# A shorter last warm-up matmul and differently cut weight loads at the head and at the first W2 chunk of a gated attention and MLP kernel

## The chip, the cores and the metric

The kernel runs on one core of a Trainium2 chip. TensorE (PE) multiplies, VectorE (DVE) and ScalarE (ACT) work on whole tiles, GpSimd (POOL) does a little, SyncE (SP) mostly issues DMA transfers; ACT and POOL can issue them too. The metric is the device time of one execution in microseconds (us). Lower is better. Times of a kernel are the median of several executions; the profile is of one further execution.

## The reference

The input x has 2048 rows (tokens) of 512 values in bf16. Two branches are computed from it and mixed row by row with a gate:

```python
g = sigmoid((x * gate_w).sum(-1))
# A: linear attention, 32 heads of 16
q, k, v = split(x @ wqkv)
phi = lambda t: where(t > 0, t + 1, exp(t)) + 1e-6
kv, z = phi(k)^T v, sum_s phi(k)           # per head
a = ((phi(q) kv) / (phi(q) z + 1e-6)) @ wo
# B: an MLP over the tokens of the layer-normed x
u = gelu(einsum("bsd,sf->bdf", layernorm(x), w1) + b1)   # F = 1792
b = (einsum("bdf,fs->bds", u, w2) + b2).transpose
out = g * a + (1 - g) * b
```

## The kernel before, in words

All operands are cut into tiles of 128 partitions: x has NT = 16 row tiles of 128 tokens, D = 512 makes ND = 4 blocks, F = 1792 makes NF = 14. A schedule written out by hand gives the order of instructions on each engine; nothing is reordered. Each engine works its own list, and semaphores hold an instruction until what it reads is there.

**The head.** SP issues the loads of x's row tiles 0 and 1 (`load_x`, L126, 128 KB each into `xs`), ACT issues parts of Wk, the middle third of wqkv (`load_wk`, L129, 128 KB for one of the four blocks k of the contraction, into `wk_sb`), and SP issues Wk's last block. x is also wanted transposed, in `xT`. Tiles 2 to 15 come transposed by DMA (`load_xT`, L132, on SP, first three single tiles, then two and three at a time); tiles 0 and 1 are transposed on TensorE (`transpose_part`, L194: matmuls `pt` of an `xs` block with the identity), and copied out of PSUM by DVE or ACT (`copy_part`, L199). Before the first block of x is there, TensorE runs `warm_up(6)` (L184, L190): six matmuls of 128x512 on a constant into the bank `wps` that nothing reads. Behind its loads, ACT has the load of its function table and a one-column exponential `act_warm` (L189).

Then the row of work on TensorE is: four `pt` of tile 0; `k_part(0, ...)` with k = 0 and 1 (`kacc`, contraction block k of x's tile times `wk_sb[:, k]`); four `pt` of tile 1; tile 0's k = 2; tile 1's k = 0 and 1; tile 0's k = 3; tile 1's k = 2 and 3; and then tile after tile.

**The rest.** For each further row tile: four `kacc` matmuls (keys), phi on ACT and DVE, and four `gacc` matmuls (Gram matrix of x and phi(k), four tiles behind). Then 16 rounds of three `uacc` (first MLP layer, W1's first chunk) and four `qacc` matmuls (queries); the remaining eleven `uacc` blocks with the small attention matrices `kvps` and `w2ps` between them; and for each output tile four `aps` and fourteen `yps` matmuls, a mix on DVE and the output transfer.

**Order of transfers.** SP's list is: x and Wk of the head, the transposed and plain tiles of x in turn, wq, W1's first chunk, wv, wo, W1's other three chunks, then W2's four chunks (`load_w2`, L432, each into a buffer of the pool `wstream` that a W1 chunk held before), then the outputs. A W2 chunk (128 x 14 x 512, 1792 KB) is issued in two halves of seven blocks of F. The first waits for the matmuls `uacc` that read W1's first chunk. Loads issued by SP and ACT count their landings on eight counters that are taken in turn.

## Time and profile before

| | us |
|---|---|
| median of three runs | 163.08 |
| lowest and highest | 162.43, 163.41 |
| profiled execution, its own time | 162.26 |
| its span, first to last instruction | 160.6 |

| stretch of the profiled execution | from, us | what TensorE does there |
|---|---|---|
| warm-ups | 0.85 | six matmuls on a constant |
| tiles 0 and 1 of x | 3.36 | transposes and first `kacc` |
| keys and Gram matrix | 6.2 | `kacc` and `gacc` in turn |
| queries and first MLP blocks | 32.3 | `uacc` and `qacc` in turn |
| other MLP blocks | 56.5 | `uacc`, with `kvps` at 63.4 and `w2ps` at 64.65 |
| outputs | 95.6 | `aps` and `yps` in turn, until 157.8 |

A line of the profile's timeline gives start, length, engine, line of the kernel, operation, output and inputs, count, and in brackets how long the engine was idle before it and what released it. "PEld" is the load of a matmul's stationary operand, and a "q" behind an engine's name (ACTq, SPq) is its queue of DMA issues: the length there is the time that the issue takes, not the transfer. The time from an issue to the landing of all its data is listed apart.

### The profile page before, as it was taken

The page shows a single profiled execution, that of the slowest core. Times are in us where ns is not written, and L with a number is a line of the kernel's source. Part 1 is how long each engine was busy: PE and PEld are TensorE (multiplying, and loading weights), DVE is VectorE, ACT ScalarE, POOL GpSimd, SP SyncE. Part 2 cuts the span into 40 slices and gives each one's busy share as a digit, 9 for nine tenths or more (in the row PEclk, how much of TensorE's full clock was granted, in tenths as well). Part 3 has the DMA queues.
Part 4 walks back from the last instruction along what each step waited for, and adds up shares of the span by engine and source line. Part 5 has one row for each costly group of instructions (what it writes and reads, how often), then busy time and mean ns, then how long its engine had stood idle before and what let it go on. Part 6 is the DMA issues. An engine that isn't in the chain of part 4 may idle for free.

```text
span 160.6 us, 2228 instructions
## 1 busy us (share of the span) xinstructions
PE 155.9 (97%) x822; PEld 72.5 (45%) x836; DVE 124.3 (77%) x274; ACT 72.7 (45%) x113; POOL 7.3 (5%) x17
## 2 busy tenths in 40 slices
PE   7999999999999999999999999999999999999993
PEld 2444444444444445444444444444444444444462
DVE  1599999769999998756999999676999999711122
ACT  3543486654978393059873320237333442111110
POOL 3000332002010000000000000000000000000000
PEclk9999999999999999999999999999999999999999
DMA  5699999999970007600930679401000001110001
GB/s 168 150 231 262 328 352 329 354 349 348 336 171 0 0 0 257 204 0 4 356 101 2 213 244 306 151 33 37 33 33 33 33 33 58 48 61 33 33 33 33
DMA packets 29929, 23.07 MB, mean 144 GB/s; under 512 B 8384, under 2 KB 29888, under 8 KB 29920
## 3 DMA queue, kind: packets, MB, share of 16 engines
q1 hardware_dynamic: 29104, 22.15, 45.2%
q10 hardware_dynamic: 704, 0.66, 1.2%
q0 software_dynamic: 112, 0.14, 0.4%
q8 instruction: 6, 0.10, 0.3%
q14 instruction: 3, 0.02, 0.0%
HBM read 19.01 MB, written 2.10 MB: 131 GB/s over the span
## 4 chain that ended last, share of the span: by engine, by line
PE 84%; DVE 13%; issue 1%; ACT 0%
PE yps L110 30%; PE uacc L110 24%; PE kacc L110 9%; PE gacc L110 9%; PE aps L110 9%; DVE pqT L213 6%; DVE zacc L274 3%; DVE stats L233 2%; DVE e L210 2%; PE wps L110 2%; PE qacc L110 1%; DVE mv L234 1%; ACT e L209 0%; PE kvps L110 0%; PE w2ps L110 0%
## 5 line engine op out<-in xcount | busy, mean ns | idle before, releaser
L110 PE MATMUL uacc<-hs,w1c 128*128 128x512 bf16 (+1 forms) x227 | 50.8, 379 | 0.4 <-issue 0.2
L110 PE MATMUL yps<-uT,w2c 128*128 128x512 bf16 (+2 forms) x247 | 50.8, 355 | 0.3
L110 PEld LDWEIGHTS <-w2c 128*128 128x128 bf16 x252 | 23.6, 98 | 25.2
L110 PEld LDWEIGHTS <-w1c 128*128 128x128 bf16 (+1 forms) x233 | 21.8, 98 | 26.0 <-issue 0.2
L488 ACT ACTIVATE a_sc<-aps,c,gg 128x512 f32<-128x512 f32 x16 | 12.4, 775 | 31.2 <-PE aps L110 15.5
L501 DVE SCALAR_TENSOR_TENSOR ot<-yps,c,a_sc 128x512 bf16<-128x512 f32 (+2 forms) x18 | 12.3, 688 | 15.3 <-PE yps L110 11.7
L322 ACT ACTIVATE uT<-uacc,bcol 128x512 bf16<-128x512 f32 x14 | 9.3, 686 | 17.5 <-PE uacc L110 17.4
L110 PE MATMUL qacc<-xT,wq_sb 128*128 128x512 bf16 x64 | 16.4, 379 | 0.1
L110 PE MATMUL aps<-W2sb,pqT 128*128 128x512 bf16 x63 | 16.4, 379 | 0.1
L110 PE MATMUL kacc<-wk_sb,xT 128*128 128x512 bf16 x63 | 15.9, 379 | 0.2 <-DVE xT L205 0.2
L387 DVE STREAM_TRANSPOSE zT<-pz 128x512 f32<-128x512 f32 x16 | 11.3, 705 | 6.0 <-ACT pz L386 6.0
L110 PE MATMUL gacc<-pk,xs 128*128 128x512 bf16 x63 | 15.7, 379 | 0.1
L249 ACT ACTIVATE hs<-xs,nmr,rstd 128x512 bf16<-128x512 bf16 x16 | 12.8, 805 | 2.3 <-DVE nmr L243 2.3
L209 ACT ACTIVATE e<-kacc 128x512 bf16<-128x512 f32 x16 | 9.4, 594 | 9.7 <-PE kacc L110 8.5
L386 ACT ACTIVATE pz<-pqT,zcol 128x512 f32<-128x512 bf16 x16 | 11.4, 715 | 4.8 <-DVE ot L501 4.7
L209 ACT ACTIVATE e<-qacc 128x512 bf16<-128x512 f32 x16 | 9.5, 594 | 7.7 <-PE qacc L110 7.7
L396 DVE STREAM_TRANSPOSE rex<-rd 128x512 bf16<-128x512 bf16 x16 | 11.4, 711 | 0.6
L213 DVE SCALAR_TENSOR_TENSOR pqT<-qacc,e 128x512 bf16<-128x512 f32 x16 | 11.1, 692 | 0.6
L213 DVE SCALAR_TENSOR_TENSOR pk<-kacc,e 128x512 bf16<-128x512 f32 x16 | 11.1, 692 | 0.6
L389 DVE TENSOR_REDUCE den<-zT 128x32 f32<-128x512 f32 x16 | 11.0, 686 | 0.6
L210 DVE TENSOR_SCALAR e<-e 128x512 bf16<-128x512 bf16 x32 | 9.0, 282 | 2.5 <-ACT e L209 2.5
L233 DVE BATCH_NORM_STATS2 stats<-xs 128x6 f32<-128x512 bf16 x16 | 10.9, 683 | 0.0
(58 smaller groups left out, 96.2 us busy)
## 6 DMA issues: line engine op xcount, KB each, us to landing
w2c<-in_B_w_dram SPq DMA_DIRECT2D x8, 896.0 KB, 5.7
w1c<-in_B_w_dram SPq DMA_DIRECT2D x3, 2048.0 KB, 14.0
out_dram<-ot SPq DMA_DIRECT2D x13, 128.0 KB, 1.7
xs<-in_A_x_dram SPq DMA_DIRECT2D x1, 1024.0 KB, 6.6
w1c<-in_B_w_dram SPq DMA_DIRECT2D x1, 1024.0 KB, 15.3
xs<-in_A_x_dram SPq DMA_DIRECT2D x1, 512.0 KB, 5.0
wq_sb<-in_A_wqkv_dram SPq DMA_DIRECT2D x1, 512.0 KB, 5.6
wv_sb<-in_A_wqkv_dram SPq DMA_DIRECT2D x1, 512.0 KB, 12.3
```

The costliest lines, as they stand in the source:

```text
L110: nc.tensor.matmul(o, lhsT=lhsT, rhs=rhs, start=start, stop=stop, **kw)
L209: nc.scalar.activation(out=e[:], in_=acc[:], func=ACT.Exp)
L210: nc.vector.tensor_scalar(out=e[:], in0=e[:], scalar1=1.0, scalar2=PHI_EPS, op0=ALU.min, op1=ALU.add)
L213: nc.vector.scalar_tensor_tensor(out=dst, in0=acc[:], scalar=0.0, in1=e[:], op0=ALU.max, op1=ALU.add)
L233: nc.vector.bn_stats(out=stats[:], in_=xs[:, t, :])
L249: nc.scalar.activation(out=hs[:, t, :], in_=xs[:, t, :], func=ACT.Identity, scale=rstd[:, t : t + 1], bias=nmr[:, t : t + 1],)
L386: nc.scalar.activation(out=pz[:], in_=seg, func=ACT.Copy, scale=zcol[:, j : j + 1])
L387: nc.vector.transpose(out=zT[:], in_=pz[:])
L389: nc.vector.tensor_reduce(out=den[:], in_=zT[:].rearrange("p (a d) -> p a d", d=HEAD), op=ALU.add, axis=AX.X)
L396: nc.vector.transpose(out=rex[:].rearrange("p (a d) -> p a d", d=HEAD), in_=rd[:].unsqueeze(2).to_broadcast([P, SC // HEAD, HEAD]),)
L488: nc.scalar.activation(out=a_sc[:], in_=aps[:], func=ACT.Identity, scale=gg[:, t : t + 1], bias=c2[:, t : t + 1],)
L501: nc.vector.scalar_tensor_tensor(out=ot[:, :W], in0=yps[:, :W], scalar=c1[:, t : t + 1], in1=a_sc[:, cs], op0=ALU.mult, op1=ALU.add,)
```

## The change

Three edits. The first two blocks of Wk, one load of 256 KB on ACT's queue, become two loads of 128 KB, with a load of x's tile 1 (on SP) between them in program order; the order of the other two Wk loads in the text is swapped, and they are on different queues. The sixth warm-up matmul has 256 columns instead of 512. The first W2 chunk is loaded in one piece of 14 blocks.

```diff
     load_x(nc.sync, 0, 1)
-    load_wk(nc.scalar, 0, 2)
+    load_wk(nc.scalar, 0, 1)
     load_x(nc.sync, 1, 1)
+    load_wk(nc.scalar, 1, 1)
+    load_wk(nc.sync, 3, 1)
     load_wk(nc.scalar, 2, 1)
-    load_wk(nc.sync, 3, 1)
     for t in (2, 3, 4):
         load_xT(t, 1)
...
-    warm_up(6)
+    warm_up(5)
+    warm_up(1, SC // 2)
...
         w2c.append(w)
-        for f0 in (0, NF // 2):
-            f1 = f0 + NF // 2
+        n = NF if c == 0 else NF // 2
+        for f0 in range(0, NF, n):
+            f1 = f0 + n
```

The order of instructions on every engine is otherwise the same, with one load more at the head of ACT's list and one less among SP's W2 loads. Since the counters are taken in turn, each load behind the new one uses the next counter, and from the W2 loads on the numbering is as before.

## The prediction

> **What bounds the kernel now.** I read the totals first.

> ```profile
> span 160.6 us, 2228 instructions
> PE 155.9 (97%) x822; PEld 72.5 (45%) x836; DVE 124.3 (77%) x274; ACT 72.7 (45%) x113; POOL 7.3 (5%) x17
> ```

> TensorE is busy for 155.9 of 160.6 us, and the chain of waits agrees: PE holds 84% of it. DVE's 13% lie between 33.8 and 55.5 us, where PE is busy for 23.84 us of the 24 between 32 and 56, so PE is not held up there either. In the chain 20 gacc matmuls take 4.32 us and 14 yps matmuls 3.02 us: 0.216 us each, end to end. So the kernel is one gapless row of matmuls, and time can be won or lost only before that row closes up, or after it. The second view is therefore the timeline of PE at the head (start, length, work; in brackets the idle time before).

> ```profile
> 0.85 2.72 PE L110 MATMUL wps<-const-bfloat16-1.0 128*128 128x512 bf16 x6 [0.85 <-PEq L522]
> 3.36 0.53 PE L110 MATMUL pt<-ident,xs 128*128 128x128 bf16 x4
> 4.06 0.60 PE L110 MATMUL kacc<-wk_sb,xT 128*128 128x512 bf16 x2 [0.17 <-DVE xT L205]
> 4.50 0.39 PE L110 MATMUL pt<-ident,xs 128*128 128x128 bf16 x4
> 4.72 1.63 PE L110 MATMUL kacc<-wk_sb,xT 128*128 128x512 bf16 x6
> ```

> The weight loads, copies and issues of the same stretch, then the transfers (KB each and median us from issue to landing; the last line is for the two x loads):

> ```profile
> 3.19 0.53 PEld L110 LDWEIGHTS <-xs 128*128 128x128 bf16 x4 [0.53 <-DMA xs<-in_A_x_dram]
> 4.05 0.29 PEld L110 LDWEIGHTS <-xT 128*128 128x128 bf16 x2 [0.34 <-DVE xT L205]
> 4.32 0.39 PEld L110 LDWEIGHTS <-xs 128*128 128x128 bf16 x4
> ...
> 3.71 0.49 DVE L205 CAST xT<-pt 128x128 bf16<-128x128 f32 x2 [1.48 <-PE pt L110]
> 4.76 0.62 DVE L205 CAST xT<-pt 128x128 bf16<-128x128 f32 x2 [0.56 <-PE pt L110]
> ```

> ```profile
> 0.81 0.98 ACTq L129 DMA_DIRECT2D wk_sb<-in_A_wqkv_dram  x2
> 1.73 0.42 SPq L129 DMA_DIRECT2D wk_sb<-in_A_wqkv_dram  x1
> 2.20 5.26 SPq L132 DMA_TRANSPOSE xT<-in_A_x_dram  x4
> ...
> 1.82 1.28 ACT L189 ACT_TABLE_LOAD   x1 [1.82 <-issue]
> 3.11 0.20 ACT L189 ACTIVATE act_warm<-ones_f 128x1 f32<-128x1 f32 x1
> 3.93 0.38 ACT L203 ACTIVATE xT<-pt 128x256 bf16<-128x256 f32 x1 [0.61 <-PE pt L110]
> ```

> ```profile
> wk_sb<-in_A_wqkv_dram ACTq DMA_DIRECT2D x1, 256.0 KB, 3.1
> xs<-in_A_x_dram SPq DMA_DIRECT2D x2, 128.0 KB, 2.7
> wk_sb<-in_A_wqkv_dram ACTq DMA_DIRECT2D x1, 128.0 KB, 3.3
> wk_sb<-in_A_wqkv_dram SPq DMA_DIRECT2D x1, 128.0 KB, 3.3
> ...
> DMA to landing us min/median/max: 2.3/2.7/3.0
> ```

> The reader is to see three things. First, the sixth warm-up starts at 2.93 and, at the 0.43 us that its fellows stand apart, hands over at 3.36, though x's first block let the weight load go at 3.19. Second, landings come in order of issue: x0 0.81+2.3 = 3.11; Wk0-1 0.81+3.1 = 3.91; x1 1.27+3.0 = 4.27; Wk2 1.30+3.3 = 4.60; Wk3 1.73+3.3 = 5.03. In bytes: 128 KB at 3.11, 384 at 3.91, 512 at 4.27, 640 at 4.60, 768 at 5.03, so 0.33 to 0.43 us for each 128 KB; the engines are saturated (374 GB/s from 2.80 to 3.20). Third, Wk2 lands at 4.60 and is used at 4.72: it has 0.12 us to spare.

> **Part 1, the half warm-up.** It removes 256 of 512 columns: 0.43/2 = 0.21 us, so the sixth ends at 3.14 and the first transpose waits for x0's weight load at 3.19. How soon a matmul follows a load that nothing covers: 0.01 us where the load at 5.10 is followed by kacc at 5.11, 0.03 at the very first pair (0.82, 0.85), and no more than a whole slow load, 0.15. I take 0.03, the pair in the same slow stretch: first transpose at 3.22, 0.14 us earlier (bounds 0.02 and 0.17). The four transposes, the DVE copy and its weight load follow, so the first kacc could go at 4.06-0.14 = 3.92, and ACT's copy at 3.93-0.14 = 3.79.

> **Part 2, Wk in three loads on ACT's ring.** ACT issues three for two: 0.46 us for the first (until 1.27), 0.49 for the second (1.30), and the third, Wk2, at 1.79 instead of 1.30. The table load behind them slides by 0.49 to 2.31-3.59 and act_warm to 3.60-3.80: under ACT's copy at 3.79 but for 0.01, and it would cost only if the table load became slower. SP's order is unchanged: x0, x1, Wk3, then the transposing loads. New on SP: loads take eight completion counters in turn, so the ninth waits for the first. With one more load at the head that is now the third single-tile xT load (L132), waiting for Wk0. It was issued at 4.84 and Wk0 lands by 3.91, so nothing; behind it stand the rest of x, wq and W1, which would all be late if it did wait. From there each SP load waits for the one eight earlier, as before.

> Issue times now: Wk0 and x0 0.81, x1 1.27, Wk1 1.30, Wk3 1.73, Wk2 1.79. If landings keep that order and the byte table above holds: x0 3.11; Wk0 (256 KB) halfway from 3.11 to 3.91, 3.51; x1 (384) 3.91; Wk1 (512) 4.27; Wk3 (640) 4.60; Wk2 (768) 5.03. A landing lets an instruction go about 0.05 us later (x1: 4.27, load at 4.32). Walk PE: first kacc 3.92 (Wk0 is there). Second kacc wants 3.92+0.23 = 4.15, but Wk1 gives 4.32; before it started at 4.29. The lead of 0.14 is gone. Tile 1's transposes 4.32+0.22 = 4.54 (x1 is there), kacc for k=2 wants 4.76 but Wk2 gives 5.08 where before it went at 4.72. Then tile 1's first kacc, which has to wait for its DVE copy until 5.11+0.03 anyway, follows at 5.08+0.22 = 5.30: 0.19 us later than 5.11. Wk3, needed next at 5.73, has long landed; xT's tile 2 (2.20+3.5 = 5.7) is wanted at 6.2+0.19. From here PE has no gap that could take the 0.19 up, so it reaches the end.

> Bounds: the order of Wk1 against x1 (0.03 us apart in issue) and of Wk2 against Wk3 (0.06 apart) decides. If Wk1 and Wk2 come first in each pair, they land at 3.91 and 4.60; kacc goes at 4.15, x1 at 4.27 lets tile 1's transposes go at 4.37, k=2 at 4.65, and tile 1's first kacc at 5.11-0.14 = 4.97: the whole 0.14 stays (0.17 at the bound). If each order goes wrong and the extra load costs a further step of 0.05, the loss is 0.25. I take the order of issue, since all five landings of before keep it.

> **Part 3, first W2 chunk in one load.** One SP issue less (0.4 to 0.56 us) at 59.97. Its halves landed in 4.6 and 6.8 us; as one load of 1792 KB it lands in no more than W1's 2048 KB took, 14.0 us, so by 74. The first yps matmul is at 96.25: 22 us cover it; only a landing later than 96 would cost. The next issue on SP waits for uacc until 74.86 in any case. I take nothing, at both ends.

> **Sum** against the profiled execution, 162.26 us (span 160.6, 1.66 around it): +0.19 + 0 + 0 = 162.45. That execution is 0.82 below the median of the runs, 163.08; the same +0.19 there gives 163.27, forecast as 163.3.

> **The clock.** The row of granted clock shows full speed throughout, but the durations don't: warm-ups stand 0.43 us apart, later matmuls 0.216; tile 0's transposes take 0.53 us, tile 1's 0.39. So TensorE went from half to full pace between 3.6 and 4.06, some 2.8 to 3.2 us after its first matmul. [...]

> **Rivals.** (B) The lead survives. For it: Wk1 and x1 are issued within 0.03 us, Wk2 and Wk3 within 0.06. Also, where the pace switches over 1 us later, kacc takes 0.43 each, k=2 is wanted only after 5.1, and Wk2's landing hides. Against it: five of five landings in order of issue. It gives 162.26-0.14 = 162.12, by the runs 162.9.
> (C) The clock switches late: the slower one. Place: the hand-over at 3.14, where PE now pauses before x0, and again at 4.15 and 4.76 for Wk. It decides if these pauses (0.08+0.17+0.32 us) leave the stretch too idle for full pace. Price: another slow stretch of 2.8 to 3.2 us at half pace loses 1.4 to 1.6; with 1.5, 163.76, by the runs 164.6. For it: the runs of before already differ by 0.98 us (162.43 to 163.41), as a wandering switch would make them. Against it: the later two pauses come after the switch of the trace, and the first takes 0.08 us of about 3.
> (D) The change has no effect, 163.1: both halves cancel. It is the middle between A and B, and counted with them.

> **Numbers.** A difference under 0.5% (0.82 us) can't be told from none. A, the forecast, 0.54; B 0.30; C 0.16. Spread of the runs lets A fall 0.02 faster, 0.48 same, 0.04 slower; B 0.05, 0.25, 0; C 0, 0.04, 0.12. Together: faster 0.07, same 0.77, slower 0.16. A and B with their spread reach from 162.4 to 163.9, and leaving out most of C keeps it within 2 in 10.

> **What would show it.** Right: first transpose at about 3.22; an idle time of PE before the second kacc and a longer one before k=2, ended by a load of wk_sb; tile 1's first kacc near 5.30; the spacing 0.216 from there; W2's one load landed by 74. B: no wait on wk_sb, tile 1's first kacc near 4.97. C: matmuls 0.43 us apart beyond 5.5. Wrong altogether: PE waits for xT or hs later on, or a changed row after 60 us.

## The result and the profile after

The changed kernel takes 164.58 us in the median of 22 runs (163.14 to 165.61) against 162.77 of 22 (162.24 to 163.44) for the kernel before: a ratio of 1.0088, with a 95% interval of 1.0061 to 1.0115. (The ratios here and below lie near those of the means; the two medians alone give 1.0111.) It is slower. The medians hide the form: eleven of the runs lie between 163.14 and 164.09, eleven between 165.07 and 165.61, and none between. I call them the lower and the upper group; the kernel before has only one. So there are two losses to explain: some 0.6 us in the lower group (its median is 163.36), and 2 us more in the other half of the runs.

The profiled execution belongs to the lower group; at 163.14 us it is the fastest of all 22. Totals and chain of waits of the changed kernel, from its page:

```profile
span 161.3 us, 2242 instructions
PE 157.3 (98%) x836; PEld 72.6 (45%) x836; DVE 124.3 (77%) x274; ACT 72.7 (45%) x113; POOL 7.3 (5%) x17
...
PE 96%; DMA 2%; DVE 0%; issue 0%
```

The span grew by 0.7 us, and a DMA has come into the chain: the page's next line names the load of x, at 2%. The head of the changed kernel on the timeline of PE, and the weight loads there:

```profile
0.85 2.51 PE L110 MATMUL wps<-const-bfloat16-1.0 128*128 128x512 bf16 x6 [0.85 <-PEq L525]
3.66 0.61 PE L110 MATMUL pt<-ident,xs 128*128 128x128 bf16 x4 [0.31 <-DMA xs<-in_A_x_dram]
4.33 1.03 PE L110 MATMUL kacc<-wk_sb,xT 128*128 128x512 bf16 x2
5.16 0.46 PE L110 MATMUL pt<-ident,xs 128*128 128x128 bf16 x4
5.60 1.71 PE L110 MATMUL kacc<-wk_sb,xT 128*128 128x512 bf16 x7
```

```profile
3.66 0.34 PEld L110 LDWEIGHTS <-xs 128*128 128x128 bf16 x4 [1.00 <-DMA xs<-in_A_x_dram]
5.84 0.55 PEld L110 LDWEIGHTS <-xT 128*128 128x128 bf16 x4 [0.34 <-DVE xT L207]
```

The reader is to see that the first transpose starts at 3.66, not at 3.36 as before or 3.22 as forecast, because x's first block lands only at 3.62. Tile 0's k=2 starts at 5.60 (before 4.72), and tile 1's first kacc at 5.84 (before 5.11). That shift of 0.73 is the 0.7 by which the span grew, so nothing after it matters. What held that kacc back to the last was the copy of tile 1's transposes by DVE (the second weight load above), late because x was late and because nearly all of TensorE's work up to there ran at the slow pace. The first two kacc take 1.03 us together, where they took 0.60 before: TensorE is still at its slow pace there, which the profile of before had left by then. The transfers of the changed kernel (KB each, median us from issue to landing), the first three issued before 2.1 us, the last from the page:

```profile
wk_sb<-in_A_wqkv_dram ACTq DMA_DIRECT2D x3, 128.0 KB, 3.2
xs<-in_A_x_dram SPq DMA_DIRECT2D x2, 128.0 KB, 2.9
wk_sb<-in_A_wqkv_dram SPq DMA_DIRECT2D x1, 128.0 KB, 3.4
```

```profile
w2c<-in_B_w_dram SPq DMA_DIRECT2D x1, 1792.0 KB, 7.6
```

The three ACT loads took 3.0, 3.2 and 3.8 us; the last of them, Wk2, issued at 1.74, landed at 5.56. W2's one load, issued at 60.7, landed by 68.3 and was wanted at 97.0.

### The profile page after: what moved, and what is told of

The parts are those of the page before. It is cut to its first block, busy times and chain, and to the rows that moved or that the text cites. A ratio compares the mean times of both kernels' runs of the same rounds, so it can differ in the third digit from the quotient of the medians.

```text
span 161.3 us, 2242 instructions
## 1 busy us (share of the span) xinstructions
PE 157.3 (98%) x836; PEld 72.6 (45%) x836; DVE 124.3 (77%) x274; ACT 72.7 (45%) x113; POOL 7.3 (5%) x17
## 4 chain that ended last, share of the span: by engine, by line
PE 96%; DMA 2%; DVE 0%; issue 0%
PE uacc L110 30%; PE yps L110 30%; PE kacc L110 9%; PE qacc L110 9%; PE gacc L110 9%; PE aps L110 9%; DMA xs<-in_A_x_dram 2%; PE kvps L110 0%; PE pt L110 0%; PE w2ps L110 0%; DVE ot L504 0%; DVE xT L207 0%; PE pt L330 0%
## 5 line engine op out<-in xcount | busy, mean ns | idle before, releaser
L110 PE MATMUL uacc<-hs,w1c 128*128 128x512 bf16 (+1 forms) x233 | 51.5, 379 | 0.0
L110 PE MATMUL yps<-uT,w2c 128*128 128x512 bf16 (+2 forms) x252 | 51.0, 355 | 0.0
L110 PEld LDWEIGHTS <-w2c 128*128 128x128 bf16 x252 | 23.6, 98 | 25.2
L110 PEld LDWEIGHTS <-w1c 128*128 128x128 bf16 (+1 forms) x233 | 21.8, 98 | 26.0 <-issue 0.2
L110 PE MATMUL kacc<-wk_sb,xT 128*128 128x512 bf16 x64 | 16.4, 387 | 0.1
L110 PE MATMUL aps<-W2sb,pqT 128*128 128x512 bf16 x64 | 16.4, 379 | 0.0
L110 PE MATMUL qacc<-xT,wq_sb 128*128 128x512 bf16 x64 | 16.4, 379 | 0.0
L110 PE MATMUL gacc<-pk,xs 128*128 128x512 bf16 x64 | 15.8, 379 | 0.0
L110 PEld LDWEIGHTS <-xs 128*128 128x128 bf16 x72 | 7.0, 101 | 8.9 <-DMA xs<-in_A_x_dram 1.0
## 6 DMA issues: line engine op xcount, KB each, us to landing
out_dram<-ot SPq DMA_DIRECT2D x13, 128.0 KB, 1.7
```

The lines of the kernel that those rows point to most:

```text
L110: nc.tensor.matmul(o, lhsT=lhsT, rhs=rhs, start=start, stop=stop, **kw)
```

## The experiments

Blocks of Wk are counted from 0, so Wk2 is the third. The number of runs stands with each time. The kernel before was run beside each group of experiments and had medians of 162.64 to 162.93. The changed kernel was not, but for the single run of e10, and the groups ran on different chips (e1 to e4; e5 to e8; e9 to e11; e12); whether the share of upper runs differs from chip to chip was not tested.

**The three edits one by one.** e1 has the half warm-up alone, e2 Wk's cut alone, e3 W2's single load alone; the diff shows the three in this order.

```diff
-    warm_up(6)
+    warm_up(5)
+    warm_up(1, SC // 2)
...
-    load_wk(nc.scalar, 0, 2)
+    load_wk(nc.scalar, 0, 1)
     load_x(nc.sync, 1, 1)
+    load_wk(nc.scalar, 1, 1)
+    load_wk(nc.sync, 3, 1)
     load_wk(nc.scalar, 2, 1)
-    load_wk(nc.sync, 3, 1)
...
-        for f0 in (0, NF // 2):
-            f1 = f0 + NF // 2
+        n = NF if c == 0 else NF // 2
+        for f0 in range(0, NF, n):
+            f1 = f0 + n
```

> The kernel before with the half-length sixth warm-up alone; Wk's and W2's loads as before. Theory L (late x): in the changed kernel x's first block landed at 3.62 us instead of 3.15, because Wk is cut in two, and TensorE then paused for 0.5 us; so this edit alone leaves the first transpose at 3.19 to 3.22 and the time at 162.6 to 162.8, with no runs near 165. Rival H (the half warm-up itself makes the clock switch late): about half of the runs lie 2 us above the others, median above 163.5.

> The kernel before with Wk's loads cut as in the change, and nothing else. Theory L: x's first block lands near 3.6 us, the first transpose starts there, TensorE pauses some 0.25 us after six full warm-ups (to 3.36), and the time is 163.1 or more, part of the runs 2 us higher since the clock switches late. Rival H: x's landing makes 0.2 us at most, 162.9 to 163.0, no runs near 165. My forecast's step (Wk1 and Wk2 land late): +0.19, also 163.0, with x landing at 3.15.

> The kernel before with the first W2 chunk in one load, and nothing else. Theory L and rival H: no difference, ratio within 0.2% of 1, the load landed by 74 us. A rival that this load, or the counters that it shifts, delays something: over 163.2.

e1: 162.69 us (162.21 to 163.49, 11 runs), ratio 1.0011 (0.9996 to 1.0027). e2: 163.64 (163.44 to 165.39, 7 runs), 1.0073 (1.0044 to 1.0102), one run of the seven in the upper group. e3: 162.98 (162.47 to 163.64, 12 runs), 1.0021 (1.0004 to 1.0038), just past the 0.2% that I had set, with an interval that leaves out 1; in its profile tile 1's first kacc comes 0.25 later than before and the span is 0.3 longer, so what it lost there was lost at the head, which the edit doesn't touch. From that kacc to the end of the span it took 155.50 us, the kernel before 155.45. The weight load of x's first block in e1 and in e2:

```profile
3.19 0.34 PEld L110 LDWEIGHTS <-xs 128*128 128x128 bf16 x4 [0.53 <-DMA xs<-in_A_x_dram]
```

```profile
3.62 0.13 PEld L110 LDWEIGHTS <-xs 128*128 128x128 bf16 x2 [0.97 <-DMA xs<-in_A_x_dram]
```

With Wk's loads as before, x is there at 3.19 and the half warm-up hands over at once: H falls, as that edit alone makes neither a loss nor an upper group, nor a gain that can be measured. (Its first transpose came 0.17 us earlier than before, its first kacc only 0.03, at 4.03, because Wk's first load landed at 3.99.) With Wk cut, x is late by 0.43. But the upper group, which holds half of the changed kernel's runs, has only one of e2's seven: a hint that it needs more than the cut, and with so few runs no more than a hint. In e3's profile x was late too, 3.53, with the head of the kernel before: so a late x occurs there also.

**Filling the pause before x.** e4 is the changed kernel with seven full warm-ups.

```diff
-    warm_up(5)
-    warm_up(1, SC // 2)
+    warm_up(7)
```

> The changed kernel with seven full warm-ups, which last until about 3.79 us and so cover the pause before x. Theory L with the clock: the pause is what puts the switch off, so the runs near 165 vanish; the first transpose starts at 3.8 and the median is 163.0 to 163.5. If late loads of x and Wk alone cost the time, whatever TensorE does meanwhile: the median stays near 164.6, in two groups.

163.62 (163.34 to 163.86, 5 runs), 1.0058 (1.0045 to 1.0071): no run in the upper group, though the loads are those of the change and there is more work. That speaks for L, that what TensorE does while it waits matters, though five runs are few. The lower group's loss is still there, and the median lies just above the 163.0 to 163.5 of L.

**Making the pause longer.** e5 is the kernel before with `warm_up(4)`, e6 the changed kernel with `warm_up(5)` and no half one.

> The kernel before with four warm-ups instead of six; all loads as before. They end at 2.5 us, so TensorE pauses 0.7 us before x's first block at 3.15 to 3.2. Theory P (a long enough pause before x puts the clock's switch off, whatever makes the pause): part of the runs, half or more, lie near 165, though x and Wk land on time. Rival: the split loads are needed for the slow group; then this stays at 162.5 to 163.5 in one group, since the same work follows at 3.2 us.

> The changed kernel with five warm-ups, without the half one: the pause before x grows from 0.5 to 0.7 us. Theory P: nearly all runs lie at 165 or above (before: 11 of 22), and a profile of such a run shows matmuls 0.43 us apart until 8 us or later. Rival (the slow group is not set by the pause): again about half of the runs at 163.3 and half at 165.3.

e5: 164.19 (163.40 to 164.59, 6 runs), 1.0080 (1.0048 to 1.0112). e6: 165.14 (163.55 to 165.44, 6 runs), 1.0118 (1.0074 to 1.0161), four of six in the upper group. So a pause alone costs over 1 us with the loads of before, against the rival; but it makes no upper group, against P. And four of six in e6 doesn't tell P (nearly all) from its rival (half). e6's profile caught a run of that group (165.07). Its timeline of PE:

```profile
0.84 2.29 PE L110 MATMUL wps<-const-bfloat16-1.0 128*128 128x512 bf16 x5 [0.84 <-PEq L524]
3.52 0.61 PE L110 MATMUL pt<-ident,xs 128*128 128x128 bf16 x4 [0.39 <-DMA xs<-in_A_x_dram]
4.19 1.03 PE L110 MATMUL kacc<-wk_sb,xT 128*128 128x512 bf16 x2
5.02 0.63 PE L110 MATMUL pt<-ident,xs 128*128 128x128 bf16 x4
5.86 5.46 PE L110 MATMUL kacc<-wk_sb,xT 128*128 128x512 bf16 x16 [0.21 <-DMA wk_sb<-in_A_wqkv_dram]
```

Sixteen kacc take 5.46 us where at 0.216 they would take 3.5. Their starts stand 0.43 us apart until 9.65 and 0.216 after. There are three pauses: before x, before the first kacc, and before k=2, which waits for Wk.

**What delays x.** e7 puts ACT's function table and `act_warm` ahead of its Wk loads; e8 cuts ACT's three blocks of Wk as one and two instead of two and one, with no load more; the diff is that of e8.

```diff
     load_x(nc.sync, 0, 1)
-    load_wk(nc.scalar, 0, 2)
+    load_wk(nc.scalar, 0, 1)
     load_x(nc.sync, 1, 1)
-    load_wk(nc.scalar, 2, 1)
+    load_wk(nc.scalar, 1, 2)
```

> The kernel before with ACT's function table and its first exponential ahead of its two Wk loads, so that these are issued at about 2.3 us instead of 0.8: x's first block travels without Wk beside it. Theory C (company of Wk's first load delays x): x lands before 3.05 us, and Wk's first load near 4.8, so the first kacc is late by 0.7 and the time over 163. Rival (x's landing has nothing to do with Wk): x lands at 3.15 to 3.5 as in the other profiles.

> The kernel before with ACT's two Wk loads cut as one block and two blocks, instead of two and one; no load more than before. Theory C with small first load: one block's packets start to flow earlier than those of a two-block load, so x lands at 3.4 to 3.6 as in the three profiles with the split, and the time is 163 to 163.6. Rival (it takes the additional load): x lands at 3.15 and the time is 162.6 to 162.9.

e7, one run: 162.51. ACT's part of its timeline:

```profile
0.80 1.28 ACT L138 ACT_TABLE_LOAD   x1 [0.80 <-PEq L522]
0.98 0.95 ACTq L129 DMA_DIRECT2D wk_sb<-in_A_wqkv_dram  x2
```

Its Wk loads went out from 0.98 on, not at 2.3 (the table load did not hold them back), so Wk was in time and the expected price did not arise; but with Wk later by 0.17 us x's weight load went at 3.02, the earliest of all. e8: 162.84 (162.63 to 163.45, 12 runs), 1.0008 (0.9987 to 1.0028). Its x is late:

```profile
3.49 0.35 PEld L110 LDWEIGHTS <-xs 128*128 128x128 bf16 x4 [0.83 <-DMA xs<-in_A_x_dram]
```

So x follows theory C and the time follows the rival. In all nine profiles with a first Wk load of one block that weight load starts at 3.41 to 3.67; with two blocks at 3.19, 3.19, 3.23 and, once, 3.53. The traces show one trait of the small first load: ACT's queue moves its first packet at 1.83 to 2.27 us in these nine, at 2.34 to 2.56 in the others. That this is what delays x is argued, not shown; the x of 3.53 was late with a first packet at 2.34. And e8 shows what a late x costs by itself under six full warm-ups: no more than 0.28% (0.46 us) by its interval, and no upper group.

**Helping without touching a transfer.** e9 is the changed kernel with one more matmul of the warm-up kind, whose result nothing reads, ahead of tile 0's k=2. e10 is the changed kernel again, for a second profile.

```diff
         for k0, k1 in ((0, 1), (1, 2), (2, ND)):
             ...
+        if t == 1:
+            warm_up(1)
         k_part(0, range(2) if t == 0 else (2,))
```

> The changed kernel with one more useless matmul of 128x512 on the constant, put after tile 1's transposes, ahead of tile 0's k=2, where TensorE waits for Wk's third block (from 5.4 to 5.85 us at the slow pace). It adds work and brings no transfer forward. [...] Rival (only late data count, work can't help): two groups as before, or later by 0.2.

> The changed kernel once more, unchanged, for a second profile. [...]

e9: 163.56 (163.31 to 163.89, 7 runs), 1.0042 (1.0027 to 1.0056), no run of seven in the upper group. With more useless work the median was lower by about 1 us (ratio 1.0042 against 1.0088), which the theory that only late data count has no place for. But e11 below, on the same chip, has only three upper runs of twelve, and in e9's own profile the pace doubled at 4.28, ahead of the added matmul at 4.83, so that profile doesn't show the matmul at work. e10 took 163.67 us; its timeline of PE and the end of its chain of waits at the head:

```profile
3.60 0.60 PE L110 MATMUL pt<-ident,xs 128*128 128x128 bf16 x4 [0.25 <-DMA xs<-in_A_x_dram]
4.28 0.61 PE L110 MATMUL kacc<-wk_sb,xT 128*128 128x512 bf16 x2
4.72 0.39 PE L110 MATMUL pt<-ident,xs 128*128 128x128 bf16 x4
6.04 4.05 PE L110 MATMUL kacc<-wk_sb,xT 128*128 128x512 bf16 x18 [0.93 <-DMA wk_sb<-in_A_wqkv_dram]
```

```profile
1.71 0.03 issue
1.74 4.26 DMA wk_sb<-in_A_wqkv_dram
5.99 0.04 issue
6.04 2.97 PE kacc L110 x13
```

This is the lower group's loss where Wk2 makes it. Here the full pace came early (tile 1's transposes take 0.39, as before), and it gained nothing: k=2 then stood until 6.04 for Wk2, issued at 1.74 and landed at 6.00. Tile 1's first kacc comes 0.22 later at 6.25, 1.14 after the 5.11 of before; the span is longer by 1.1.

**Wk2 sooner.** e11 swaps the queues of Wk's third and fourth block; e12 puts both on SP, ahead of the transposing loads. The diff is that of e11; in e12 the last line has `nc.sync` too.

```diff
-    load_wk(nc.sync, 3, 1)
-    load_wk(nc.scalar, 2, 1)
+    load_wk(nc.sync, 2, 1)
+    load_wk(nc.scalar, 3, 1)
```

> The changed kernel with Wk's third block on SP's queue and its fourth on ACT's, instead of the other way round; all else as in the change. [...] Rival (Wk2's landing plays no part in the slow group): still half of the runs near 165.3.

> The changed kernel with Wk's third and fourth block both on SP's queue, in that order, ahead of the transposing loads of x; ACT issues only the first two blocks. The third block is issued at 1.73 us, as when it alone was put on SP (landing then 5.72), but the transposing loads start 0.46 us later, at 2.66. Theory T (Wk's third block lands late, at 5.56 to 6.0 instead of 4.61, because its packets run beside those of the transposing loads): it lands before 5.1, the pause before k=2 vanishes, and the fast group lies at 162.6 to 163.2, with at most a quarter of the runs near 165. Rival (the late landing comes from the three loads of one block each, whatever runs beside them): it lands at 5.5 or later and the fast group stays at 163.3.

e11: 163.38 (163.04 to 165.45, 12 runs), 1.0048 (1.0019 to 1.0076), three of twelve in the upper group. Wk2 took 4.0 us from 1.73 and landed at 5.7, no earlier than in the changed kernel, so the swap did not do what it was to test, and three of twelve against eleven of 22 says little. e12: 163.29 (162.68 to 163.67, 12 runs), 1.0028 (1.0011 to 1.0045), none in the upper group. Its Wk2 landed at 1.75+3.7 = 5.47, later than the 5.1 of theory T and nearer to the rival's 5.5, and the lower group was at the rival's 163.3; but the pause before k=2 was gone in its profile, since TensorE was slow then and came to k=2 only at 5.61:

```profile
5.18 0.63 PE L110 MATMUL pt<-ident,xs 128*128 128x128 bf16 x4
5.61 3.62 PE L110 MATMUL kacc<-wk_sb,xT 128*128 128x512 bf16 x13
```

Theory T as I put it is not borne out. Wk2 lands by 4.6 to 5.1 with five loads of x and Wk at the head, at 5.47 to 6.0 in all eight profiles with six, at each of the three places where it was put. Part of this is the issue, at 1.73 to 1.75 instead of 1.24 to 1.44; the rest is the way from issue to landing, 3.7 to 4.3 us instead of 3.3 to 3.7. Why one load more makes that way longer stayed open.

**All profiles together.** The row of granted clock stands at full in all of them (0.999 or 1.0 over each profiled run); the pace has to be read from the starts of the matmuls: 0.427 us apart, then 0.216. For each profile, when the pace doubled, and the sum of TensorE's pauses from its first matmul up to that point, worked out from the starts:

| kernel | x's weight load | k=2 starts | pace doubles | pauses up to there | runs in the upper group |
|---|---|---|---|---|---|
| before | 3.19 | 4.72 | 3.65 | 0.0 | 0 of 22 |
| changed | 3.66 | 5.60 | 5.30 | 0.8 | 11 of 22 |
| e1 half warm-up | 3.19 | 5.26 | 5.29 | 0.5 | 0 of 11 |
| e2 Wk cut | 3.62 | 5.84 | 5.37 | 0.5 | 1 of 7 |
| e3 W2 in one | 3.53 | 4.98 | 4.39 | 0.5 | 0 of 12 |
| e4 seven warm-ups | 3.47 | 5.91 | 5.31 | 0.3 | 0 of 5 |
| e5 four, loads as before | 3.23 | 5.18 | 6.85 | 1.0 | 0 of 6 |
| e6 five, loads changed | 3.52 | 5.86 | 9.65 | 1.3 | 4 of 6 |
| e7 | 3.02 | 5.15 | 3.94 | 0.2 | 0 of 1 |
| e8 | 3.49 | 5.27 | 4.42 | 0.4 | 0 of 12 |
| e9 filled | 3.41 | 5.92 | 4.28 | 0.5 | 0 of 7 |
| e10 changed | 3.60 | 6.04 | 4.29 | 0.7 | 0 of 1 |
| e11 | 3.58 | 5.76 | 9.51 | 0.9 | 3 of 12 |
| e12 | 3.67 | 5.61 | 6.92 | 0.8 | 0 of 12 |

The doubling came anywhere from 3.65 to 9.65, and in the two profiles of the changed kernel, with first transposes at 3.66 and 3.60, at 5.30 and 4.29. (In e10 the long pause before k=2 came after the doubling and is not in the sum.) In the nine profiles with pauses of 0.7 us or less the pace had doubled by 5.37; in the five with 0.8 or more it doubled at 5.30 once and else at 6.85 to 9.65. That order was read off these profiles, and a late doubling also lets more pauses into the sum; no run was made to test it, and how long or how steadily TensorE has to work before its pace doubles was not shown. The changed kernel itself has no profile of an upper run; those of e6 and e11 stand for it.

The counts of upper runs, from which that order was not read, can be set against it, and fit it in part. The upper group has 4 of 6 runs of e6, whose pauses sum to 1.3, 3 of 12 of e11 (0.9), 11 of 22 of the changed kernel (0.8, and 0.7 in e10) and 1 of 7 of e2 (0.5). Of the 69 runs of the kernel before, e1, e3, e4, e8 and e9, with 0.5 or less, it has none. But it has none either of the 12 of e12 (0.8) or of the 6 of e5 (1.0), which spread over 163.40 to 164.59. So the sum of the pauses alone doesn't decide which kernels have upper runs.

What lies behind the head adds nothing else. From tile 1's first kacc to the end of the span it is 155.4 to 155.5 us in nine of the ten profiles whose pace had doubled by 5.4 (155.7 in e2), 155.9 and 156.1 where it doubled near 6.9, and 157.1 in e6 and e11. The 1.66 us more than in the kernel before (155.45) are what the slow pace cost in those two.

## Why the prediction was wrong

**The landing of x, held at 3.11,** is the step that failed first. The landings kept the forecast order in the changed kernel's profile, but not the times of the byte table: 3.62, 3.81, 4.21, 4.44, 5.18 and 5.56 instead of 3.11, 3.51, 3.91, 4.27, 4.60 and 5.03. The table moved only Wk and x's second tile and took x's first from before; the runs put x's weight load at 3.41 to 3.67 wherever the first Wk load has one block. The warm-ups ended at 3.14 as forecast, so the pause before x was 0.52 us instead of 0.08, and Part 1's gain of 0.14 became a loss of 0.30 in the first transpose.

**Wk2's landing** was the right mechanism with the wrong size. The walk had k=2 wait for Wk2 from 4.76 to 5.08, and tile 1's first kacc at 5.30: the term of +0.19. In seven of the eight profiles with six loads k=2 starts 0.04 after Wk2's landing. In e10 Wk2 landed at 6.00, not 5.03, and tile 1's first kacc came at 6.25: +1.14 for +0.19. In the other profile of the changed kernel, its fastest run, the path was another: Wk2 at 5.56 held k=2 for 0.14, but tile 1's first kacc waited for DVE's copy anyway, and its +0.73 came from the late x (0.30) and from transposes and kacc at the slow pace (the rest). The byte table was the fault here too: it took one load more of the same bytes as free. With 256 KB cut into two, the runs show 3.7 to 4.3 us from Wk2's issue to its landing instead of 3.3 to 3.7. The second kacc's wait for Wk1, forecast from 4.15 to 4.32, did not show: with x late that kacc was wanted only at 4.73 and, in e10, at 4.50, and Wk1 had landed at 4.44 and 4.35.

**Rival C was what decided**, and I had given it 0.16; the sum had nothing for it. Its place was right by what the runs show, pauses at the head and a full pace that comes late: with the loads of before, e5's longer pause went with a doubling at 6.85 instead of 3.65, and the three pauses of e6 went with one at 9.65. Its price of 1.5 was somewhat low: the slow pace costs 1.66 in the profiles, and the groups lie some 2 us apart. That its 164.6 is the measured median is luck: no run lies between 164.09 and 165.07, and the median falls there because the halves are equal. It was set aside with the argument that the first pause "takes 0.08 us of about 3", which fell with x's landing, and that "the later two pauses come after the switch of the trace". That switch, at 3.65, was that of one execution, and one of the fastest: 162.26, where the 22 runs of before begin at 162.24. In the profile of e6 the pauses measure about 0.6, 0.3 and 0.4 us, all of them ahead of the doubling. The half warm-up alone put 0 of 11 runs in the upper group, the cut alone 1 of 7, both together 11 of 22, and with the first pause (0 of 5) or the third (0 of 7) filled it was empty. The counts are small and of different chips; e5, whose loads are those of before, is the better ground for the pauses, but it has no upper run.

**Rival B and its 0.14** did not occur: x was late. **Part 3** held: landed by 68.3, and the profile of that edit alone shows no loss behind the head (155.50 us against 155.45); its runs were slower by 0.04 to 0.38%, which the edit is not shown to cause. ACT's act_warm and the third xT load (issued at 4.84, as before) cost nothing, as forecast.

**The range** of 162.4 to 163.9 was built around one group; the upper group, half of the runs, carried the median past it. That the lower group's median, 163.36, meets the forecast of 163.3 is luck as well: the forecast added 0.19 to 163.08, the median of three runs, where 22 runs of before gave 162.77 and the loss was 0.59.

## What to carry to other kernels

At the head of a kernel the pauses of TensorE are to be summed, not costed one by one: each may be covered, and yet with 1.3 us of them together the full pace came only at 9.65 in e6, where in the kernel before, with none up to there, it came at 3.65. Before a load is cut in two, ask what the further load does to the landings beside it, the one that TensorE waits for first among them. And a spare matmul at the end of a warm-up may be an insurance against a late landing, as the runs of e4 suggest; a trace with an early landing doesn't show its worth.
